# A hand-laid order of steps for pooled attention and an MLP mixer, laid out anew for units 0 to 7

## The chip, the cores and the metric

The kernel runs on one core of a Trainium2 chip. The metric is the device time of one execution in microseconds; three executions give a median. The profile is of one further execution.

## The reference

Eight batches, eight heads, 576 rows, head dimension 64. Keys and values are first averaged over groups of 8 rows (72 groups), then attention runs over the 72 pooled rows. The result, laid out as 576 x 512 for each batch, goes through a mixer: a token part (576 to 256 to 576 along the rows) with a residual, then a channel part (512 to 1536 to 512) with a residual.

```python
k_p = k.reshape(B, H, Sp, 8, D).mean(axis=3);  v_p = v.reshape(B, H, Sp, 8, D).mean(axis=3)
attn = softmax(scale * q @ k_p.T)                      # 576 x 72 for each head
x = (attn @ v_p) as (B, 576, 512)
h = relu(x.T @ w_tok1) @ w_tok2;   u = x + h.T         # token part
out = u + relu(u @ w_ch1) @ w_ch2                      # channel part
```

## The kernel before, in words

All engines are driven from one list of steps that was written out by hand, and the order in which the program issues instructions is the order in which each engine runs them (`tc.manual_schedule`). There is a head (the string `HEAD`) that loads weights and batch 0, computes batch 0's attention and warms TensorE, and then nine units, 0 to 8. Unit n computes the channel part of batch n for 512 of its 576 rows; unit 8 does the remaining 64 rows of all eight batches together.

A unit is a generator (`unit_fast`) that issues a little TensorE work and yields, 45 times in units 0 to 6. Yields 0 to 23 are the first layer (`l1_tile`, L551): 12 tiles of four 512-column matmuls, two for each yield, each tile evicted by ScalarE with a ReLU into `GT` (L555). Yields 24 to 44 are the second layer in seven products of 12 matmuls of 256 columns (L699), three yields each. They follow a scheme with seven instead of eight block products: VectorE forms sums of blocks of `GT` (steps `=1` to `=4`, L579 and L594, into the tile `area`), and, once in unit 0, sums of blocks of `w_ch2` (steps `w0` to `w3`, L579, into `area2`, which the trace also calls area). The products are, in order, x, y, z, x again (needs `=1` to be read by z, and `=2`), w, z again (needs `=4`), x a third time (needs `=3` and `w2`). Each ends in VectorE adds (L742, tiles `s` and `o`); the x, y, z, w banks are four one-bank PSUM tiles, `p1a` to `p1d`, taken and given back in turn, and the steps below share them. Units 7 and 8 do the first layer in a seven-product scheme too (`l1_fast`, L672), with sums of `w_ch1` (steps `Z0` to `Z3`, on POOL) and of the transposed u (steps `y` on VectorE, `Y` on POOL).

`PLAN[n]` says which steps of later batches are issued after which yield of unit n. A step is written batch dot name:

- `lq`, `lk`, `lv`: POOL issues the load of q, k, v of that batch (L162, L124). Raw tiles have two buffers each.
- `K0 K1 V0 V1`: POOL pools half of the heads of k or v in three adds (L208, L209, L212 or L214). `k0 k1 v0 v1`: the same on VectorE.
- `1.vpool0`, `1.vpool1`: batch 1's values are pooled by six matmuls each (L144, `add_rows`; batch 1 is in `WIDE`, six rows for each partition), and cast by VectorE (L295).
- `Q0 Q1`: VectorE transposes q (`qD`, L312). `kpT`: TensorE transposes the pooled keys (L256), ScalarE copies them (L258).
- `s0 s1 s2`: scores (L325) into both buffers of the two-bank PSUM tile `p`, exponentials on ScalarE (L334).
- `av0` to `av4`: attention times values (L413) into one buffer of `p`; VectorE takes reciprocals (L417) and scales (L356). `aw`: the same with the scaling on ScalarE in eight pieces (L360).
- `at0 at1`: the token part's first layer (L425, ReLU L427). `u0` to `u4`: its second layer (L447, `u4` L442) and the residual add on VectorE (L448). `t0` to `t3`: transposes of u on TensorE (L456, copy L457) for the first layer of the next unit.
- From batch 3 on the transposes go another way: `M0 M2 M4` spill u to HBM from SP's queue (L466), `M` and `MT` read it back in another order (L478), and `T0` to `T5` are block transposes on VectorE (L490).
- `g`: a gate. VectorE writes a flag (L865) and POOL copies it (L866), so POOL does not go on before VectorE has come to that place. There is one flag, so VectorE's next gate also waits until POOL has copied the last one.

Of the kernel before, what the change touches and what calls it, by code (L numbers as in the profile page):

```python
# [19 lines left out]

HEAD = """LkA LkT LkB LvT Lq LvA LvB Lt1 Lk1 Lt2 Lc1b Lc1a Lq1 Lc1c Lv1 Lc1d p1 Lc2a Lc2b Lc2c d2 d2 d3 d1 d4 d4 c0 c1 prep q0 kp0 kp1 kt0 q1 d1 o0 kt1 kp2 e0 e1 q3 kt2 o1 q2 e3 vpool0 o3 e2 a00 vpool1 a02 o2 m01 d1 d1 m00 a04 X1 m03 a14 m02 X0 m04 p0 a10 a12 1.kpool m10 m14 m12 m13 m11 A1 A0 X2 X3 A2 A3"""
PLAN = [
# [9 lines left out]
]  # L32

# [907 lines left out]
```

## Time and profile before

| | |
|---|---|
| median of 3 runs | 262.4 us (262.34 to 263.7) |
| the profiled execution | 261.59 us, span 259.8 us |
| PE (TensorE) busy | 253.5 us (98%) |
| DVE (VectorE) busy | 195.3 us (75%) |
| ACT (ScalarE) busy | 125.1 us (48%) |
| POOL (GpSimd) busy | 159.2 us (61%) |
| mean granted TensorE clock | 0.997 |
| first matmul of units 0 to 8 | 23.65, 55.64, 85.75, 113.47, 142.91, 167.19, 194.03, 218.63, 237.00 us |

The busy time of PE counts matmuls whose ends are modelled and overlap the next, so it is read here for gaps only. A row of the timeline gives start, length, engine, line, operation, tile written from tiles read, and in brackets the idle time of the engine before it and what ended it.

### The profile page before, as it was taken

The numbers are of one execution on the slowest core, as the hardware profiler recorded it, in microseconds if no ns is written. First come the engines' busy times: TensorE is split into PE (matmuls) and PEld (weight loads), VectorE is DVE, ScalarE is ACT, GpSimd is POOL, SyncE is SP. The second block draws the span as 40 slices with busy tenths as digits, with TensorE's granted clock in tenths as the row PEclk, the third lists the DMA queues.
The fourth block names the chain that finished last, engine by engine and source line by source line (L and its number), as shares of the span: only waits on it lengthen the run. The fifth ranks groups of instructions, "written<-read, shape, count | busy, mean of one in ns | idle before, by whom it ended". The sixth has DMA issues, their size and how long they took to land.

```text
span 259.8 us, 5518 instructions
## 1 busy us (share of the span) xinstructions
PE 253.5 (98%) x2187; PEld 167.2 (64%) x2187; DVE 195.3 (75%) x400; ACT 125.1 (48%) x229; POOL 159.2 (61%) x166
## 2 busy tenths in 40 slices
PE   8999999999999999999999999999999999999994
PEld 2885456764676645774487447754784478888883
DVE  5557469995789747789799548944795389999993
ACT  3354874059746565466741575065525421623610
POOL 8757226999989999389969962898308913100000
PEclk9999999999999999999999999999999999999998
DMA  7999999994090989479834942930405042503304
GB/s 153 192 201 207 205 207 209 206 225 87 3 174 7 165 192 200 124 132 237 200 109 78 216 170 61 158 97 1 159 20 149 30 146 61 172 0 68 97 3 161
DMA packets 31930, 34.31 MB, mean 132 GB/s; under 512 B 2976, under 2 KB 23968, under 8 KB 31904
## 3 DMA queue, kind: packets, MB, share of 16 engines
q0 software_dynamic: 17856, 17.64, 43.2%
q1 hardware_dynamic: 13632, 15.93, 20.5%
q10 hardware_dynamic: 416, 0.39, 0.5%
q8 instruction: 17, 0.28, 0.4%
q14 instruction: 9, 0.07, 0.1%
HBM read 38.99 MB, written 12.58 MB: 199 GB/s over the span
## 4 chain that ended last, share of the span: by engine, by line
PE 92%; DVE 5%; issue 1%; ACT 0%; DVEq 0%; ACTq 0%
PE p1a L699 8%; PE p1c L551 8%; PE p1d L699 7%; PE p1a L551 7%; PE p1b L699 7%; PE p1b L551 7%; PE p1d L551 7%; PE p1c L699 5%; PE p L413 4%; PE p L325 3%; PE p L672 2%; PE p1d L425 2%; PE p1c L447 2%; PE p1b L425 2%; PE p1b L144 1%; DVE s L742 1%
## 5 line engine op out<-in xcount | busy, mean ns | idle before, releaser
L551 PEld LDWEIGHTS <-w_ch 128*128 128x128 bf16 x336 | 30.2, 98 | 34.0 <-issue 3.0
L699 PEld LDWEIGHTS <-area 128*128 128x128 bf16 x432 | 41.3, 98 | 7.9 <-issue 1.0
L334 ACT ACTIVATE ex<-p 72x768 bf16<-72x768 f32 x42 | 31.6, 803 | 16.1 <-PE p L325 16.1
L866 POOL COPY flag<-flag 1x1 f32<-1x1 f32 x35 | 10.2, 292 | 47.1 <-DVE flag L865 46.9
L699 PEld LDWEIGHTS <-GT 128*128 128x128 bf16 x312 | 29.6, 98 | 7.0 <-issue 1.8
L209 POOL TENSOR_TENSOR t<-t 72x512 f32<-72x512 f32 x22 | 31.0, 1411 | 1.7
L551 PE MATMUL p1c<-uT,w_ch 128*128 128x512 bf16 x92 | 24.9, 379 | 0.0
L208 POOL TENSOR_TENSOR t<-vr 72x1024 f32<-72x1024 bf16 x11 | 24.0, 2181 | 0.6
L208 POOL TENSOR_TENSOR t<-kr 72x1024 f32<-72x1024 bf16 x11 | 24.0, 2178 | 0.3
L551 PE MATMUL p1a<-uT,w_ch 128*128 128x512 bf16 x84 | 22.6, 380 | 0.0
L551 PE MATMUL p1d<-uT,w_ch 128*128 128x512 bf16 x80 | 22.3, 379 | 0.0
L551 PE MATMUL p1b<-uT,w_ch 128*128 128x512 bf16 x80 | 21.5, 379 | 0.0
L356 DVE TENSOR_TENSOR x<-p,den 128x512 bf16<-128x512 f32 x28 | 19.4, 692 | 1.0
L555 ACT ACTIVATE GT<-p1a 128x512 bf16<-128x512 f32 x21 | 12.7, 605 | 14.3 <-issue 7.2
L555 ACT ACTIVATE GT<-p1c 128x512 bf16<-128x512 f32 x23 | 13.9, 603 | 8.1 <-PE p1c L551 8.1
L555 ACT ACTIVATE GT<-p1b 128x512 bf16<-128x512 f32 x20 | 12.1, 604 | 8.8 <-PE p1b L551 5.2
L413 PEld LDWEIGHTS <-ex 72*128 72x128 bf16 x280 | 12.8, 98 | 5.3 <-DVE xt L356 0.7
L555 ACT ACTIVATE GT<-p1d 128x512 bf16<-128x512 f32 x20 | 12.0, 600 | 6.9 <-PE p1d L551 6.1
L579 DVE TENSOR_TENSOR area<-GT 128x1536 bf16<-128x1536 bf16 x9 | 11.0, 1218 | 5.6 <-ACT AT L427 5.1
L413 PE MATMUL p<-vp,ex 72*128 72x65 bf16 x280 | 14.0, 194 | 0.2 <-DVE xt L356 0.2
L448 DVE TENSOR_TENSOR u<-p1c,x 128x512 bf16<-128x512 f32 x11 | 8.0, 730 | 7.9 <-PE p1c L447 7.6
L594 DVE TENSOR_TENSOR area<-GT 128x1536 bf16<-128x1536 bf16 x9 | 9.1, 1016 | 6.1 <-ACT GT L555 5.8
(244 smaller groups left out, 550.3 us busy)
## 6 DMA issues: line engine op xcount, KB each, us to landing
out_dram<-o SPq DMA_DIRECT2D x32, 256.0 KB, 4.1
qb<-in_q_dram POOLq DMA_DIRECT2D x7, 576.0 KB, 10.8
kr<-in_k_dram POOLq DMA_DIRECT2D x6, 512.0 KB, 10.7
vr<-in_v_dram POOLq DMA_DIRECT2D x6, 512.0 KB, 11.7
w_ch<-in_moe_w_ch_dram POOLq DMA_DIRECT2D x5, 512.0 KB, 16.5
mem<-u SPq DMA_DIRECT2D x10, 256.0 KB, 2.2
v<-mem SPq DMA_DIRECT2D x20, 128.0 KB, 2.8
area<-in_q_dram SPq DMA_DIRECT2D x2, 288.0 KB, 3.1
```

Of the source, the lines that this page charges most:

```text
L208: eng.tensor_tensor(out=t4[:, 0:n], in0=t[:, hs, 0:4], in1=t[:, hs, 4:8], op=ALU.add)
L209: eng.tensor_tensor(out=t4[:, 0:n, 0:2], in0=t4[:, 0:n, 0:2], in1=t4[:, 0:n, 2:4], op=ALU.add)
L334: nc.scalar.activation(out=dst, in_=src, func=AF.Exp, scale=scale)
L356: nc.vector.tensor_tensor(out=dst, in0=view, in1=den[:, :, :, None].broadcast_to([n, a, 4, D]), op=ALU.mult)
L413: nc.tensor.matmul(out=ps[:, h // 4, (h % 4) * (D + 1):(h % 4 + 1) * (D + 1)], lhsT=st["ex"][:, h * S + n0:h * S + n0 + P], rhs=st["vp"][: ...
L425: nc.tensor.matmul(out=ps, lhsT=w_tok1[:, c if c < 4 else 4 + par, m * P:(m + 1) * P], rhs=st["x"][:, c, :] if c < 4 else st["xt"], start= ...
L551: nc.tensor.matmul(out=ps, lhsT=w_ch1[:, kk, m * P:(m + 1) * P], rhs=uT[kk], start=(kk == 0), stop=(kk == 3))
L555: nc.scalar.activation(out=GT[:, :, m, :], in_=ps.rearrange("p (h n) -> p h n", h=2), func=AF.Relu)
L579: eng.tensor_tensor(out=out, in0=a, in1=b, op=ALU.subtract)
L594: eng.tensor_tensor(out=S[0], in0=g[1][0], in1=g[1][1], op=ALU.add)
L699: nc.tensor.matmul(out=ps[i] if split else ps[:, i], lhsT=chunk(u, i, a(m)), rhs=w(m), start=start and m == 0 and (i == 0 or split), stop= ...
L866: nc.gpsimd.tensor_copy(out=flag[:, 1:2], in_=flag[:, 0:1])
```

## The change

`HEAD` stays, and so do all functions. The rows of `PLAN` for units 0 to 7 are replaced; unit 8's row stays. The steps are the same, in another order, but for one: the second half of the pooling of batch 7's values (`7.V1` on POOL) becomes `7.v1` on VectorE. There are 37 gates in place of 35. Some steps change the unit: `2.v1` goes from unit 1 to the end of unit 0; `3.Q0` from unit 0 to 1; `3.av0`, `4.Q0` and `5.lk` from unit 1 to 2; `4.aw2` and `6.lq` from unit 2 to 3; `7.lv`, `6.av0` and `5.u4` from unit 4 to 5.

```diff
 PLAN = [
-    {0: "0.u0 2.lk 0.u1 1.Q0 1.Q1", 2: "1.kpT", 3: "3.lq 2.lq", 5: "0.u3", 6: "1.s0", 7: "0.u2", 8: "2.lv", 9: "1.s1", 11: "1.vpool1", 12: "1.s2 1.vpool0", 13: "=3 g", 14: "1.av2", 15: "1.av1", 17: "1.aw0", 18: "1.av4 g", 19: "w0", 20: "3.lv 1.av3", 22: "w1", 23: "g =1 =2 3.lk", 25: "1.at1 1.at0 =4", 26: "g 2.K1", 27: "2.K0", 28: "w3", 29: "2.V0", 33: "1.u0", 34: "1.u1", 35: "1.u2", 36: "w2", 37: "2.Q1 1.t2", 40: "1.u3", 41: "1.t0", 42: "1.t3", 43: "g 1.t1 3.Q0 2.Q0 1.u4"},
-    {0: "2.kpT", 1: "2.v1", 3: "2.s0", 8: "3.K1 2.s2", 9: "3.K0", 11: "4.lq", 12: "2.s1", 15: "3.Q1", 16: "2.aw3", 17: "2.av1", 18: "g", 20: "2.av0", 21: "2.av4", 23: "2.av2 =1", 24: "4.lk", 25: "g", 26: "3.kpT 2.at1", 27: "=2", 28: "2.at0 =4 g", 31: "2.u3 4.Q1", 32: "3.s2", 33: "2.t3 2.u2", 35: "3.s0 3.V1", 36: "=3", 37: "3.V0", 38: "g 2.u1", 39: "4.lv 3.s1 2.u0", 40: "5.lk", 41: "4.Q0 2.t2 2.t0", 43: "2.t1 3.av0 3.av2"},
-    {4: "4.K1", 6: "3.av3 3.av4", 9: "3.av1 4.K0", 12: "g 3.at1", 13: "6.lk", 14: "=3 3.at0", 18: "4.kpT 4.V1", 19: "3.u1 4.V0", 20: "3.u0 3.u3", 21: "3.u2 3.u4", 23: "4.s2", 24: "3.M0 3.M2", 25: "=1", 26: "3.M4", 27: "=2", 28: "4.s0", 29: "=4", 30: "3.M", 31: "4.s1 3.MT 3.T3 3.T0", 32: "g 5.lq 5.lv", 34: "3.T1", 35: "4.av4 4.aw1", 36: "3.T2", 38: "g 6.lq", 40: "g", 42: "4.aw2 6.lv"},
-    {1: "4.av0", 3: "5.K1", 5: "4.av3", 8: "4.at1", 9: "4.at0 5.k0", 10: "5.Q0", 11: "4.u2", 12: "5.V0", 13: "4.u1", 15: "5.kpT 4.u3 5.V1", 16: "4.M2", 17: "5.s0", 18: "=3 5.Q1", 19: "6.Q0", 22: "4.u0", 23: "5.s1", 24: "4.M0", 25: "3.T4 =1 3.T5", 26: "=2", 27: "=4", 28: "g", 29: "4.M", 30: "5.s2", 32: "5.av0", 35: "5.av2", 37: "5.av1", 40: "5.av3 5.av4", 42: "4.T3 4.T1 4.T0", 43: "4.T2 5.at0 5.at1"},
-    {2: "6.K1", 5: "7.lq 7.lk 5.u3", 6: "5.u2", 8: "5.u0", 10: "6.K0", 11: "6.kpT", 12: "5.u1 6.V1 6.V0", 13: "5.M0", 16: "6.s0", 17: "5.M2", 18: "5.M", 20: "7.Q1", 21: "7.Q0", 22: "6.Q1 g", 23: "=1", 24: "6.s1 =3", 26: "g", 28: "=2", 29: "6.s2 5.T1", 30: "g", 32: "g 7.lv 5.T3", 34: "5.T0 =4", 36: "g", 37: "g", 41: "5.T2", 42: "6.av3", 44: "6.av0 5.u4"},
-    {0: "7.K0", 2: "6.av2", 6: "6.av1", 7: "6.av4", 8: "7.K1", 9: "6.at0 7.V1 g", 10: "7.kpT g", 12: "=3", 13: "6.at1 g", 14: "g", 17: "6.u3 7.V0", 18: "6.u1", 20: "g 6.u2 7.s0", 21: "6.u0", 24: "7.s1", 25: "=1", 27: "=2 6.M2", 32: "7.av1", 33: "6.M0 =4", 35: "6.M", 36: "7.s2", 37: "g", 39: "6.T0 6.T2", 40: "g", 41: "6.T3", 42: "6.T1", 44: "7.av2 g 7.av3"},
-    {1: "Z0", 4: "7.av0", 6: "7.av4", 8: "7.at1", 10: "Z1", 15: "7.at0", 16: "Z2", 17: "7.u1 7.u0 7.M0 7.u3 7.u4", 19: "7.u2", 20: "=3 Z3", 22: "7.M2", 25: "g =1", 27: "=2 7.M", 28: "g", 33: "=4", 34: "g", 35: "g 7.T3", 37: "7.T1 7.M4 7.T2", 38: "7.T0", 42: "7.y0", 43: "g 7.y1", 44: "7.Y2"},
-    {0: "g", 6: "7.MT", 12: "7.Y3", 18: "g", 21: "=1", 27: "=2", 30: "=3", 32: "=4", 34: "7.T4", 35: "7.T5", 40: "8.y0", 41: "8.y1 8.y3", 42: "8.y2"},
+    {1: "1.Q0 0.u1", 2: "1.kpT 0.u2", 3: "2.lk 2.lq", 6: "0.u0 2.lv 1.s0", 7: "1.Q1", 9: "3.lq 0.u3 1.s1", 10: "1.vpool1", 12: "g 1.s2 1.vpool0", 13: "=3", 14: "1.av1 1.av2", 15: "g", 16: "1.aw0", 17: "1.av4", 19: "w0", 20: "3.lv", 21: "1.av3", 22: "w1", 23: "g =1 =2 3.lk", 24: "g", 25: "1.at1 =4", 26: "2.K1", 27: "1.at0 2.K0", 28: "w3", 30: "2.V0", 33: "1.u0 1.u1", 34: "2.Q1 1.u2", 37: "1.t2", 40: "w2 1.u3 1.t0", 42: "1.t3", 43: "1.t1 2.Q0 g 1.u4", 44: "2.v1 g"},
+    {0: "2.kpT", 4: "2.s0", 5: "3.Q0", 8: "2.s2", 9: "3.K0", 11: "3.K1", 12: "2.s1", 13: "4.lq", 14: "g", 16: "3.Q1 2.aw3", 17: "2.av1", 20: "2.av0", 21: "2.av4", 23: "2.av2", 24: "4.lk =1", 26: "3.kpT 2.at1", 27: "=2 2.at0", 28: "g", 29: "3.V1", 30: "2.u3", 31: "=4 4.Q1", 32: "3.s2", 33: "2.t3 2.u2", 35: "=3 3.s0", 37: "3.V0", 38: "g 2.u1", 39: "3.s1 4.lv 2.u0", 41: "2.t2", 42: "2.t0 2.t1", 43: "3.av2"},
+    {0: "3.av0", 3: "4.Q0", 4: "3.av4 5.lk 4.K1", 8: "g 3.av3", 9: "4.K0", 10: "6.lk", 11: "3.av1", 15: "4.V1", 16: "3.at0 3.at1", 17: "4.V0", 18: "4.kpT =3 3.u0", 19: "3.u1 4.s1", 20: "3.u3", 21: "3.M0 3.u2", 23: "3.u4", 24: "3.M2 4.s2", 25: "=1", 26: "3.M4", 27: "=2", 28: "4.s0", 29: "3.M =4", 30: "3.T0", 32: "g", 34: "5.lq 5.lv", 35: "4.aw1 3.T1 3.T2 3.MT", 36: "4.av4", 37: "3.T3", 38: "g g", 44: "6.lv"},
+    {0: "6.lq", 3: "4.av0", 4: "5.K1 4.aw2", 5: "4.av3", 6: "5.k0", 7: "5.Q0", 8: "4.at1", 9: "4.at0", 12: "5.V0", 13: "4.u1", 15: "4.u2 5.kpT", 16: "=3", 17: "4.u3", 18: "5.Q1 5.s0", 20: "6.Q0", 22: "4.u0 5.V1 4.M0", 23: "5.s1", 24: "4.M2", 25: "3.T4 =1 3.T5", 26: "=2", 27: "=4", 28: "g", 29: "4.M", 30: "5.s2", 32: "5.av0", 34: "5.av4", 37: "5.av1", 38: "5.av2", 40: "5.av3 4.T2", 42: "4.T3 4.T0", 43: "5.at0 4.T1", 44: "5.at1"},
+    {2: "5.u0", 3: "6.K1", 8: "5.u3", 9: "6.K0 7.lq 6.V0", 10: "7.lk", 11: "6.kpT", 13: "5.u2 5.u1", 14: "6.V1", 17: "g 5.M0 5.M2", 18: "6.s0 5.M", 20: "7.Q1 =3", 21: "7.Q0 6.Q1", 24: "6.s1", 25: "=1 g", 28: "g", 29: "=2", 30: "5.T1", 31: "=4", 32: "5.T3 g 6.s2 5.T0", 34: "g", 36: "g", 42: "5.T2 6.av3"},
+    {0: "7.lv 6.av0", 1: "5.u4 6.av2", 3: "7.K0", 6: "6.av1", 7: "6.av4", 8: "7.K1", 9: "6.at0 g 7.v1", 10: "g", 13: "6.at1", 15: "g", 16: "=3 7.V0 7.kpT", 17: "6.u3", 18: "6.u1", 20: "7.s0 6.u2 g", 21: "6.u0", 23: "7.s1", 25: "=1", 27: "=2", 28: "6.M2", 32: "7.av1 g", 33: "6.M0 =4", 36: "7.s2", 37: "g", 38: "6.M", 39: "6.T0 6.T2", 40: "g", 41: "g", 42: "6.T3 6.T1", 44: "7.av2 g 7.av3"},
+    {0: "Z0", 4: "7.av0", 6: "7.av4", 8: "7.at1", 12: "Z1", 15: "7.at0", 17: "7.u1 7.u0 7.u3", 18: "Z2", 19: "7.u2", 20: "=3 Z3", 21: "7.M0 7.u4", 22: "7.M2", 23: "g", 25: "=1 7.M", 26: "=2", 28: "g", 29: "g", 31: "g", 33: "=4 g", 35: "g 7.T3", 36: "7.T0", 37: "7.T1 7.T2", 39: "7.M4", 43: "7.y0 7.y1", 44: "7.Y2"},
+    {0: "g", 2: "7.Y3", 13: "7.MT", 18: "g", 19: "=1", 28: "=2 =3", 31: "=4", 35: "7.T4", 36: "7.T5", 38: "8.y0", 41: "8.y1 8.y3", 44: "8.y2"},
     {21: "=1", 26: "=2", 29: "=4", 32: "=3"},
 ]
 
```

## The prediction

> **What bounds the kernel now.** I read the page's busy line, then the chain that ended last, then the stages.
>
> ```profile
> span 259.8 us, 5518 instructions
> PE 92%; DVE 5%; issue 1%; ACT 0%; DVEq 0%; ACTq 0%
> 23.65:55.64 31.99, 31.64 (x268) 19.43 (x267) 25.03 (x45) 17.15 (x34) 17.64 (x20) 1.00 1.23 206
> 55.64:85.75 30.11, 29.88 (x296) 18.42 (x294) 23.54 (x38) 20.69 (x40) 28.05 (x28) 1.00 0.46 86
> 237.00:259.80 22.80, 18.87 (x170) 16.33 (x167) 18.35 (x36) 7.28 (x13) 0.00 (x0) 0.97 0.32 93
> sum 236.15, PE 231.64 PEld 152.14 DVE 181.16 ACT 115.14 POOL 141.51; mean PE 25.74 PEld 16.90 DVE 20.13 ACT 12.79 POOL 15.72
> ```
>
> TensorE (PE) is 92% of the chain. The stage rows are units 0, 1 and 8 (start and end, length, then busy time of PE, PEld, DVE, ACT, POOL), the sum is over units 0 to 8: in 236.15 us PE is idle for 4.5, and 3.9 of that is unit 8, which keeps its plan. The granted clock is 1.00, so a faster array is not to be had. VectorE (DVE), 181 of 236, is the only other engine near its limit.
>
> So an order can win only where PE stands between two matmuls. I went through the starts of PE's matmuls for gaps over the usual pitch (0.216 us for 512 columns).
>
> ```profile
> 26.54 0.86 PE p1b L551 x4
> 38.24 0.59 PE L551 MATMUL p1d<-uT,w_ch 128*128 128x512 bf16 x2
> 39.00 0.43 PE L413 MATMUL p<-vp,ex 72*128 72x65 bf16 x8 [0.17 <-DVE xt L356]
> 50.59 0.40 PE L456 MATMUL p1d<-ident,u 128*128 128x128 bf16 x4 [0.18 <-DVE u L448]
> 81.95 0.59 PE L447 MATMUL p1b<-AT,w_tok 128*128 128x512 bf16 x2 [0.23 <-DVE flag L865]
> 134.10 0.43 PE L413 MATMUL p<-vp,ex 72*128 72x65 bf16 x8
> ```
>
> Four matmuls take 0.86, so two begun at 38.24 are through at 38.67, and `1.av3` begins at 39.00: 0.33 lost. In this way I count six gaps in units 0 to 7, the first at 39.00, the last at 134.10 (0.08): 0.33, 0.12, 0.34, 0.30, 0.24, 0.08, in all 1.41 us. That is the most an order of units 0 to 7 can gain: 0.54%.
>
> **The change, part by part.** The PE steps are the same set, so PE's work is the same to the matmul. One pooling changes its engine, gates go from 35 to 37, the rest is order.
>
> *`7.V1` becomes `7.v1` on DVE.* Prices: the three adds of `2.v1`. Cover: DVE's idle time ahead of `7`'s place.
>
> ```profile
> 57.15 1.81 DVE L208 TENSOR_TENSOR t<-vr 72x1024 f32<-72x1024 bf16 x1
> 59.00 1.64 DVE L209 TENSOR_TENSOR t<-t 72x512 f32<-72x512 f32 x1
> 60.67 0.83 DVE L214 TENSOR_TENSOR vp<-t 72x256 bf16<-72x256 f32 x1
> 177.85 0.95 DVE L579 TENSOR_TENSOR area<-GT 128x1536 bf16<-128x1536 bf16 x1 [5.14 <-ACT AT L427]
> ```
>
> 4.28 us go into a hole of 5.14, and the sum behind it (`=3`, now yield 16) stays near 178. Cost 0; without that hole it would delay `=3` and the u adds by 4.28, still 30 yields before `=3` is read.
>
> *Unit 0, the av steps.* `1.av1` and `1.av2` now stand together at yield 14, the next two a yield earlier.
>
> ```profile
> 35.03 0.42 PE L413 MATMUL p<-vp,ex 72*128 72x65 bf16 x8
> 36.65 0.69 DVE L356 TENSOR_TENSOR x<-p,den 128x512 bf16<-128x512 f32 x1
> ```
>
> The first begins at 35.03 as before. DVE still scales them one behind the other (second result at 37.34, the end of the row, the first 0.84 earlier), and two PSUM tiles are all there is. PE would reach `1.aw0` at 35.03 + 2 x 0.27 + 2 x 0.43 = 36.43 and `1.av4` at 37.26: it waits about 0.14 at each. `1.av3` at yield 21 finds its tile free. Net +0.28 - 0.33 = -0.05.
>
> *Unit 0, `w2` from yield 36 to 40.* This is the term that decides. What a DVE sum of two bf16 tiles does beside a POOL add is seen in unit 1:
>
> ```profile
> 78.36 2.12 POOL L208 TENSOR_TENSOR t<-vr 72x1024 f32<-72x1024 bf16 x1
> 79.16 2.14 DVE L579 TENSOR_TENSOR area<-GT 128x1536 bf16<-128x1536 bf16 x1
> 80.56 1.88 POOL L209 TENSOR_TENSOR t<-t 72x512 f32<-72x512 f32 x1
> ```
>
> The sum alone takes 0.95 (row 177.85). Here it begins 0.80 into POOL's add, gets going when that ends (80.48) and ends at 81.30; POOL's next add then waits for the sum. Now unit 0's end:
>
> ```profile
> 44.00 1.24 POOL L124 DMA_DIRECT2D kr<-in_k_dram  x2 [1.21 <-DMA kr<-in_k_dram]
> 45.42 0.83 POOL L866 COPY flag<-flag 1x1 f32<-1x1 f32 x1 [0.19 <-DVE flag L865]
> 45.26 0.95 DVE L579 TENSOR_TENSOR area<-w_ch,area 128x1536 bf16<-128x1536 bf16 x1
> 46.22 2.11 POOL L208 TENSOR_TENSOR t<-kr 72x1024 f32<-72x1024 bf16 x1
> 49.75 0.84 POOL L212 TENSOR_TENSOR kp<-t 72x256 bf16<-72x256 f32 x1
> 50.44 0.97 DVE L579 TENSOR_TENSOR area<-w_ch 128x1536 bf16<-128x1536 bf16 x1
> 50.67 2.73 POOL L208 TENSOR_TENSOR t<-kr 72x1024 f32<-72x1024 bf16 x1
> 52.02 0.65 DVE L742 TENSOR_TENSOR s<-p1c,u 128x512 f32<-128x512 f32 x1
> 53.22 0.60 PE L699 MATMUL p1a<-area,area 128*128 128x256 bf16 x4
> ```
>
> Before, `w2` (50.44) slips in between POOL's L212 (ends 50.59) and the next L208, which it delays. After, it stands behind the `s4` add (52.02, some 0.15 earlier there as two DVE instructions ahead of it are gone) and begins at 51.9. POOL's L208, no longer delayed, runs from 50.67 to 52.78. `w2` gets through at 53.6. Its reader is the last product of unit 0 (before at 53.22; after, without waits, 53.0): PE waits 0.55. Queued behind `w2` on DVE is `1.u3`'s add, for which `1.t3` then waits some 0.2 more. Bounds: 0, if `w2` meets no POOL add (row 50.44); up to 1.8, if it begins just after one of 2.1 us. I take 0.75, near the row 79.16. The trace agrees with a rule of the Trainium skill ("SBUF — State Buffer", Who interferes with whom): a VectorE instruction with two SBUF inputs and a GpSimd instruction that reads SBUF exclude each other, and whoever issues first holds the port for its whole instruction. By that rule alone the collision is certain; by row 50.44 alone unit 0 would end 0.75 earlier.
>
> The u and t steps from yield 33 lose 0.33 in place of 0.46 (row 50.59: `2.Q1` now runs before `1.u2`'s add, but `1.u1` is a yield earlier). Unit 0 in sum: -0.05 + 0.75 - 0.13, about **+0.6**.
>
> *Units 1 and 2.* `=3` of unit 1 moves up a yield and meets the end of a POOL add, not its first half; the gap at 81.95 shrinks from 0.30 to 0.1. `4.s1` leaves the end of unit 2, and with it the gap of 0.24 there. Against that, `3.T0` moves to yield 30, ahead of `s5`:
>
> ```profile
> 104.60 3.72 SPq L478 DMA_DIRECT2D v<-mem  x8
> 108.99 0.77 DVE L490 STREAM_TRANSPOSE uT<-v 128x256 uint32<-128x256 uint32 x2 [1.62 <-DMA v<-mem]
> ```
>
> DVE already waits 1.62 us here for the bounce through HBM, with `s5` behind it. `3.u2` and so the bounce come about 0.9 later, `s5` about 0.6 later, just when PE wants it; the last transpose (`3.T3`) ends as unit 3 begins. 0 to 0.6; I take 0.3. Sum -0.2 - 0.24 + 0.3, **-0.15**.
>
> *Unit 3.* `4.aw2` goes into the row `4.av0`, `4.aw2`, `4.av3` of three neighbouring yields on two PSUM tiles: 0.2. And POOL issues `6.lv` ahead of `6.lq`:
>
> ```profile
> 113.31 0.72 POOL L162 DMA_DIRECT2D qb<-in_q_dram  x1
> 114.15 1.27 POOL L124 DMA_DIRECT2D vr<-in_v_dram  x2
> 126.38 1.43 DVE L312 STREAM_TRANSPOSE qD<-qb 128x576 uint32<-128x576 uint32 x2
> 128.72 0.73 DVE L448 TENSOR_TENSOR u<-p1b,x 128x512 bf16<-128x512 f32 x1 [0.91 <-PE p1b L447]
> DMA to landing us min/median/max: 6.7/9.3/11.9
> ```
>
> The last row is of the two q loads in this stretch; 113.31 + 11.9 = 125.2, and `6.Q0` is the second of the transposes at 126.38. Issued 2.3 us later and behind v, `6.lq` lands near 129, and DVE stands at `6.Q0` for 1.5 us, with `4.u0`'s add, `=1`, `=2`, `=4` and the av scalings behind. Ahead of that add DVE is idle for 0.91 now (row 128.72), so some 0.6 of the 1.5 is left as delay on DVE, which is then busy up to the unit's end; it comes to PE through the av tiles and the last transposes of the unit, and I take 0.4 (0 to 1.2). With two small gaps of before gone (0.15), **+0.45**.
>
> *Loads and spills.* In unit 0 POOL issues `2.lq` and `2.lv` ahead of `3.lq`; `3.lk` still comes last and still waits for `2.lk`'s landing (row 44.00, 1.21), so POOL's first pooling of batch 2 can begin no earlier. `2.lv` lands sooner and `3.lq` later, both far ahead of use. In unit 3 SP gets `4.M0` ahead of `4.M2` and waits at it for `4.u0`; the bounce comes 0.4 later with some 4 us to spare. 0.
>
> *Units 4 to 7.* `6.K0` and `6.V0` come earlier, batch 5's tail (`5.u4`) moves from unit 4 into unit 5 with its work; every gate's POOL copy is done before DVE's next gate writes the flag. I find no wait: 0, with -0.2 to +0.3.
>
> Sum: 0.6 - 0.15 + 0.45 = 0.9, against the profiled execution of 261.59 us (span 259.8 and 1.8 around it): 262.5. The median of the three runs, 262.4, lies 0.8 above that execution; on it the forecast is **263.2 us** (0.8 of the 0.9 taken, as the small terms are rounded up).
>
> **The rivals.**
> 1. *POOL takes the port first (slower).* POOL's issue of `3.lk` ends at 44.00 + 1.24 = 45.24. In the new order gate and `2.K1` stand ahead of `w3`, whose DVE queue reaches it near 45.14. If the load lands 0.15 earlier, or DVE comes 0.15 later, `2.K1`'s L208 begins first and `w3` waits until 47.5; `oa`, `s5` and three u adds queue behind, and PE, which needs their PSUM tiles from 47.4 on, loses about 1.4 there and 1.0 at `w2`, less the 0.2 that the other terms of unit 0 save; with 0.3 from units 1 to 3, +2.5: 264.9. For it: a margin of 0.1 us. Against: before, the copy at 45.42 was held by `w3` in just this way. The skill's same section says that issue order decides who blocks.
> 2. *The new waits are absorbed.* `w2` finds a gap, or `6.lq` lands in time: -0.2, 262.2.
> 3. *The order does what an order can.* All gaps but a tenth go: 262.4 - 1.3 = 261.1. Against it: the rows of `w2`.
> 4. *The bounce in unit 2 comes a full 1 us late*, and unit 3 cannot begin: +1.6, 264.0.
>
> **How the numbers follow.** Forecast 0.40 (262.5 to 264.2), rival 1 0.25 (264 to 266), rival 2 0.20, rival 3 0.08, rival 4 0.07. A half per cent is 1.3 us, about what a measurement of this kernel can tell from no change; so faster means under 261.1, slower over 263.7. Faster: most of rival 3, 0.06. Slower: rival 1, most of rival 4, and a fifth of the forecast, 0.39. The rest, 0.55, is the same. Range 261.4 to 265.4: it leaves out the far ends of rivals 1 and 3. Without rival 1 the forecast's own range is 262.5 to 264.2.
>
> **What would show it.** Right: in unit 0 a row DVE L579 near 51.9 of 1.5 us or more, and PE's last product there after 53.5; in unit 3 the second qD transpose waiting for a DMA near 128; unit 4 beginning 0.5 to 1.2 us later. Rival 1: L579 near 45.2 over 2 us. Wrong: unit 0 ending before 55.64, or a new PE gap in units 4 to 7, where I found none.

## The result, and the profile after

| | before | after |
|---|---|---|
| median of 18 runs each on the same chip | 262.10 us (261.59 to 263.70) | 264.42 us (262.87 to 269.66) |
| the profiled execution | 261.59 us, span 259.8 | 264.25 us, span 262.5 |

The changed kernel takes 1.0081 times as long, 95% interval 1.0058 to 1.0104, that is 2.1 us more; the ratios here and below leave disturbed runs out (of the changed kernel's 18 the three from 267.55 us up, whose granted clock was 0.991 to 0.994). It is slower by more than the half per cent that the prediction set as its line. The other 15 lie between 262.87 and 266.31 us, a wider spread than before. Below, before and after name the two kernels, and a row is quoted by its start.

The chain that ended last in the changed kernel, then its stages: units 0 to 5 and the sum over all nine units (start and end, length, then busy time of PE, PEld, DVE, ACT, POOL).

```profile
PE 71%; DMA 13%; DVE 9%; issue 3%; POOL 2%; ACT 0%; DVEq 0%; ACTq 0%; POOLq 0%
```

```profile
23.51:58.47 34.96, 32.48 (x263) 19.16 (x266) 26.63 (x44) 17.06 (x34) 19.07 (x21) 1.00 1.17 195
58.47:88.10 29.63, 29.36 (x283) 18.16 (x286) 20.73 (x37) 20.69 (x40) 26.53 (x28) 1.00 0.43 81
88.10:115.60 27.50, 27.34 (x238) 16.79 (x239) 19.92 (x38) 14.78 (x29) 22.65 (x22) 1.00 0.79 167
115.60:145.62 30.02, 29.65 (x259) 17.90 (x260) 26.53 (x50) 14.86 (x30) 24.27 (x19) 1.00 0.63 140
145.62:168.98 23.36, 23.31 (x184) 14.46 (x185) 15.83 (x35) 12.22 (x20) 13.56 (x19) 1.00 0.66 143
168.98:196.73 27.75, 27.59 (x245) 17.05 (x246) 22.34 (x48) 12.95 (x21) 16.04 (x17) 1.00 0.38 97
sum 238.95, PE 231.46 PEld 151.51 DVE 185.00 ACT 115.38 POOL 138.19; mean PE 25.72 PEld 16.83 DVE 20.56 ACT 12.82 POOL 15.35
```

The same view of the kernel before, units 2 to 5 (units 0 and 1 stand in the prediction):

```profile
85.75:113.47 27.72, 27.72 (x240) 16.87 (x238) 19.57 (x37) 14.07 (x28) 22.34 (x22) 1.00 0.78 160
113.47:142.91 29.44, 29.44 (x255) 17.77 (x252) 26.20 (x50) 15.48 (x34) 25.81 (x21) 1.00 0.76 162
142.91:167.19 24.28, 24.28 (x197) 14.91 (x197) 16.39 (x36) 11.90 (x20) 15.76 (x18) 1.00 0.66 143
167.19:194.03 26.84, 26.84 (x236) 16.75 (x235) 17.72 (x43) 13.03 (x21) 15.82 (x18) 1.00 0.28 80
```

Compare lengths, not busy times (the trace of after lacks 24 matmul records). Unit 0 lasts 34.96 in place of 31.99: **+2.97**. Units 1 to 3 together -0.12 (-0.48, -0.22, +0.58; two av steps of 0.27 moved from unit to unit among them). Units 4 and 5 trade a step and batch 5's tail: -0.92 and +0.91. Units 6 and 7 are equal and unit 8 is 0.04 shorter. So the 2.7 us between the two profiled executions are unit 0.

Inside unit 0, the timeline of after:

```profile
41.85 0.96 DVE L579 TENSOR_TENSOR area<-w_ch,area 128x1536 bf16<-128x1536 bf16 x1 [0.54 <-DMA w_ch<-in_moe_w_ch_dram]
44.63 0.06 DVE L865 MEMSET flag<- 1x1 f32 x1
45.06 1.25 POOL L124 DMA_DIRECT2D kr<-in_k_dram  x2 [1.32 <-DMA kr<-in_k_dram]
46.20 3.17 DVE L579 TENSOR_TENSOR area<-w_ch,area 128x1536 bf16<-128x1536 bf16 x1
46.30 0.17 POOL L866 COPY flag<-flag 1x1 f32<-1x1 f32 x1
46.44 2.11 POOL L208 TENSOR_TENSOR t<-kr 72x1024 f32<-72x1024 bf16 x1
49.29 0.68 DVE L742 TENSOR_TENSOR o<-p1b,s 128x512 f32<-128x512 f32 x1
50.02 0.59 PE L447 MATMUL p1b<-AT,w_tok 128*128 128x512 bf16 x2 [1.85 <-DVE o L742]
51.26 0.38 PE L447 MATMUL p1d<-AT,w_tok 128*128 128x512 bf16 x1 [0.21 <-DVE u L448]
54.63 1.14 DVE L579 TENSOR_TENSOR area<-w_ch 128x1536 bf16<-128x1536 bf16 x1
```

The sum `w3` takes 3.17 us where it took 0.95: it stands until POOL's L208 ends (48.55). The `o` add behind it gives a PSUM bank back 3.2 us later than before (46.13 there), and PE waits for it. This is rival 1. `w2`, the forecast's own term, is only 0.2 over: with everything before it late, it meets the last 0.3 of a POOL add.

Not all of the 2.97 is the order. In this execution the sum `w1` (row 41.85) waited 0.54 for the last load of `w_ch`, which landed 19.4 us after its issue (18.3 in the trace before); DVE, and so `w3`, came later by that. The 13% of DMA in the chain lead through this load. In f4 below, a run with the same row of `PLAN` for unit 0, `w1` did not wait, and unit 0 lasted 34.37. In f2, with the unit 0 of before, `w1` waited 0.33, so the late landing does not need the new order.

What the gate did stands in one row of the kernel before, beside the copy at 45.42 in the prediction:

```profile
45.28 0.06 DVE L865 MEMSET flag<- 1x1 f32 x1
```

There the memset stood next to `w3` on DVE, and POOL could not go on before DVE had come to it. After, the memset is done at 44.63, and only the issue of `3.lk` holds POOL.

### The profile page after: what moved, and what is told of

It is laid out like the page before. It is cut to its first block, busy times and chain, and to the rows that moved or that the text cites. A ratio compares the mean times of both kernels' runs of the same rounds, so it can differ in the third digit from the quotient of the medians.

```text
span 262.5 us, 5503 instructions
## 1 busy us (share of the span) xinstructions
PE 252.4 (96%) x2163; PEld 166.3 (63%) x2187; DVE 199.1 (76%) x405; ACT 125.4 (48%) x229; POOL 155.7 (59%) x165
## 4 chain that ended last, share of the span: by engine, by line
PE 71%; DMA 13%; DVE 9%; issue 3%; POOL 2%; ACT 0%; DVEq 0%; ACTq 0%; POOLq 0%
DMA w_ch<-in_moe_w_ch_dram 7%; PE p1b L699 7%; PE p1d L551 6%; PE p1b L551 6%; PE p1c L699 6%; PE p1c L551 6%; PE p1a L699 6%; PE p1a L551 5%; PE p1d L699 5%; DMA area<-in_moe_w_tok_dram 3%; PE p L325 3%; PE p L413 3%; DMA qb<-in_q_dram 2%; PE p L672 2%; DVE area L579 2%
## 5 line engine op out<-in xcount | busy, mean ns | idle before, releaser
L209 POOL TENSOR_TENSOR t<-t 72x512 f32<-72x512 f32 x21 | 28.5, 1359 | 1.6
L551 PE MATMUL p1b<-uT,w_ch 128*128 128x512 bf16 x90 | 24.8, 379 | 0.1
L551 PE MATMUL p1d<-uT,w_ch 128*128 128x512 bf16 x87 | 24.3, 379 | 0.2
L208 POOL TENSOR_TENSOR t<-kr 72x1024 f32<-72x1024 bf16 x11 | 23.4, 2124 | 0.4
L208 POOL TENSOR_TENSOR t<-vr 72x1024 f32<-72x1024 bf16 x10 | 21.8, 2184 | 1.4 <-DMA vr<-in_v_dram 1.0
L551 PE MATMUL p1c<-uT,w_ch 128*128 128x512 bf16 x77 | 22.0, 379 | 0.3
L356 DVE TENSOR_TENSOR x<-p,den 128x512 bf16<-128x512 f32 x28 | 19.4, 691 | 1.0
L551 PE MATMUL p1a<-uT,w_ch 128*128 128x512 bf16 x68 | 18.6, 378 | 0.1
L555 ACT ACTIVATE GT<-p1d 128x512 bf16<-128x512 f32 x23 | 13.9, 605 | 9.8 <-PE p1d L551 9.4
L448 DVE TENSOR_TENSOR u<-p1a,x 128x512 bf16<-128x512 f32 x12 | 8.7, 726 | 9.9 <-PE p1a L447 8.6
L417 DVE RECIPROCAL den<-p 128x8 f32<-128x8 f32 (+1 forms) x35 | 7.0, 200 | 9.7 <-PE p L413 9.2
L124 POOL DMA_DIRECT2D vr<-in_v_dram x15 | 9.5, 637 | 7.7 <-DMA vr<-in_v_dram 3.4
```

Source lines behind the costliest of these rows:

```text
L124: nc.gpsimd.dma_start(out=t[j0:j1, h0:h1].rearrange("j h i d -> j h (i d)"), in_=src[b, h0:h1].rearrange("h (j i) d -> j h (i d)", i=POOL) ...
L208: eng.tensor_tensor(out=t4[:, 0:n], in0=t[:, hs, 0:4], in1=t[:, hs, 4:8], op=ALU.add)
L209: eng.tensor_tensor(out=t4[:, 0:n, 0:2], in0=t4[:, 0:n, 0:2], in1=t4[:, 0:n, 2:4], op=ALU.add)
L356: nc.vector.tensor_tensor(out=dst, in0=view, in1=den[:, :, :, None].broadcast_to([n, a, 4, D]), op=ALU.mult)
L448: nc.vector.tensor_tensor(out=rows_of(c), in0=blocked(ps), in1=blocked(x), op=ALU.add)
L551: nc.tensor.matmul(out=ps, lhsT=w_ch1[:, kk, m * P:(m + 1) * P], rhs=uT[kk], start=(kk == 0), stop=(kk == 3))
```

## The experiments

All are differences in `PLAN`; steps are quoted with their yields. Medians of all runs, with the ratio to the kernel before on the same chip. Unit 0 is that of the one profiled execution:

| run | us | ratio, 95% interval | unit 0, us |
|---|---|---|---|
| e1: after, gate back at 26 | 264.01 | 1.0047 (1.0022 to 1.0072) | 33.32 |
| e2: before, gate at 24 | 263.37 | 1.0044 (1.0025 to 1.0062) | 33.29 |
| e3: after, `w2` back at 36 | 263.93 | 1.0060 (1.0037 to 1.0084) | 33.44 |
| e4: before, `7.v1` on DVE | 263.42 | 1.0038 (1.0024 to 1.0053) | 31.99 |
| f1: after, gate and `w2` back | 263.97 | 1.0057 (1.0024 to 1.0090) | 34.13 |
| g1: f1, `2.Q1` back | 262.55 | 1.0026 (0.9998 to 1.0053) | 32.65 |
| g3: before, `2.Q1` ahead of `w2` | 263.44 | 1.0038 (1.0017 to 1.0058) | 33.26 |
| h1: f1, a gate at `w2` | 262.76 | 1.0021 (1.0000 to 1.0042) | 32.02 |
| f2: before's unit 0, rest of after mended | 262.18 | 0.9996 (0.9976 to 1.0015) | 32.16 |
| f3: e4, `7.kpT` later | 262.36 | 0.9995 (0.9977 to 1.0013) | 32.00 |
| f4: after, units 3 and 4 mended | 263.77 | 1.0055 (1.0037 to 1.0073) | 34.37 |
| g2: all named steps mended | 262.38 | 0.9999 (0.9981 to 1.0017) | 32.19 |

**e2, the gate alone, in the kernel before.**

```diff
-25: "1.at1 1.at0 =4", 26: "g 2.K1",
+24: "g", 25: "1.at1 1.at0 =4", 26: "2.K1",
```

> The kernel before with only that gate moved the other way, from yield 26 to 24 of unit 0; no other step moves. Theory 1: POOL is through with the issue of 3.lk when VectorE comes to w3, the copy and 2.K1's first add go first, w3 takes about 3.1 us, and 1.2 to 2.0 us are lost: 263.3 to 264.1. Theory 2 and theory 3: no change, 262.1.

```profile
45.00 0.17 POOL L866 COPY flag<-flag 1x1 f32<-1x1 f32 x1
45.14 2.11 POOL L208 TENSOR_TENSOR t<-kr 72x1024 f32<-72x1024 bf16 x1
45.40 2.67 DVE L579 TENSOR_TENSOR area<-w_ch,area 128x1536 bf16<-128x1536 bf16 x1
48.73 0.59 PE L447 MATMUL p1c<-AT,w_tok 128*128 128x512 bf16 x2 [0.46 <-DVE o L742]
```

Two yields for one gate cost 1.0 us in the median and 1.30 in unit 0. `w3` is held as in after; `w2`, late in its turn, meets a POOL add too and takes 1.49, of which PE loses 0.24. The mechanism is shown in the kernel before, with nothing else changed.

**e1, the gate put back in the changed kernel.**

```diff
-24: "g", 25: "1.at1 =4", 26: "2.K1",
+25: "1.at1 =4", 26: "g 2.K1",
```

> The changed kernel with unit 0's second gate moved from yield 24 to 26, where it stood before: its flag is then written behind the s1 add, directly ahead of w3. Theory 1 (POOL's first add of 2.K1 takes the port ahead of w3): w3 back from 3.17 to about 0.95 us, 1.7 to 2.2 us of the loss gone, 262.2 to 262.8; then w2 at yield 40 should meet a POOL add and cost up to 0.75. Theory 2 (the loss is at w2, the forecast): no change, 264.4. Theory 3 (loads in unit 0 land later): at most 0.3 less.

```profile
46.28 0.95 DVE L579 TENSOR_TENSOR area<-w_ch,area 128x1536 bf16<-128x1536 bf16 x1
46.51 0.77 POOL L866 COPY flag<-flag 1x1 f32<-1x1 f32 x1
51.71 2.12 POOL L208 TENSOR_TENSOR t<-kr 72x1024 f32<-72x1024 bf16 x1
52.87 1.78 DVE L579 TENSOR_TENSOR area<-w_ch 128x1536 bf16<-128x1536 bf16 x1
54.70 0.60 PE L699 MATMUL p1c<-area,area 128*128 128x256 bf16 x4 [0.52 <-DVE area L579]
164.57 0.45 DVE L490 STREAM_TRANSPOSE uT<-v 128x256 uint32<-128x256 uint32 x1 [2.69 <-DMA v<-mem]
166.57 0.60 PE L699 MATMUL p1d<-w_ch,area 128*128 128x256 bf16 x4 [1.78 <-DVE s L742]
```

`w3` is clean, the copy waits for it, and unit 0 is 1.6 shorter than after's. Now the forecast's term appears as drawn: `w2` meets an L208 and takes 0.83 more, PE loses 0.68. The time gives little of it back: the median is 264.01, where 262.2 to 262.8 and up to 0.75 for `w2` were expected. The profiled execution (264.88; the runs reach from 262.30 to 266.99) shows two more losses. PE also stands 0.47 early in unit 0, and here `5.T1` (unit 4, moved ahead of `=4` and its adds) waited 2.69 us for the read-back of the bounce, whose slowest landing took 4.7 us (3.1 in after): unit 4 took 25.46 in place of 23.36. One profile does not tell how much of this is in the median.

**e3, `w2` put back, the gate left.**

```diff
-34: "2.Q1 1.u2", 37: "1.t2", 40: "w2 1.u3 1.t0",
+34: "2.Q1 1.u2", 36: "w2", 37: "1.t2", 40: "1.u3 1.t0",
```

> The changed kernel with w2 back at yield 36 of unit 0, the gate as changed. Theory 1: w3 still blocked for 3.1 us and the main loss stays; 0.0 to 0.3 us less than 264.4, as w2 met the end of a POOL add at 54.63 and took 1.14 instead of 0.95. Theory 2: 0.75 less, 263.7.

`w2` took 0.93, `w3` still 2.98. The median lies between the two theories, and its ratio cannot be told from after's. Unit 0 is 33.44, 1.5 shorter than in after, but the place of `w2` gives only 0.27 of that (PE ahead of its matmuls at 55.83 and 56.48 in after). 0.81 is a shorter wait for the bank behind `w3` (1.20 lost there, 2.01 in after, 1.46 in f4), and the rest comes earlier in the unit. The gate's collision stays.

**f1, both put back.** The edits of e1 and e3 together.

> The changed kernel with both unit 0 terms undone: the gate stands again ahead of 2.K1 at yield 26, w2 again at yield 36. Everything else of the new order stays. Theory 1 (nearly all of the loss is the two port collisions in unit 0): w3 takes 0.95 us, w2 takes 0.95 to 1.0, unit 0 lasts 32.0 to 32.5 us (34.96 in the profile of the changed kernel, 31.99 before), and the time is 262.0 to 262.6, that is within 0.2% of the kernel before. Theory 2 (the rest of the new order costs about 1 us as well): unit 0 as short, but the time 263 or more, with the loss seen in units 3 and 4.

Neither theory foresaw this: unit 0 took 34.13.

```profile
50.29 0.76 DVE L312 STREAM_TRANSPOSE qD<-qb 128x576 uint32<-128x576 uint32 x1
51.83 2.12 POOL L208 TENSOR_TENSOR t<-kr 72x1024 f32<-72x1024 bf16 x1
52.17 2.59 DVE L579 TENSOR_TENSOR area<-w_ch 128x1536 bf16<-128x1536 bf16 x1
55.41 0.38 PE L456 MATMUL p1b<-ident,u 128*128 128x128 bf16 x4 [1.54 <-DVE s L742]
```

At its old yield `w2` comes 0.34 behind POOL's start, as the transpose `2.Q1` (0.76) stands ahead of it; before, that stood behind. So there is a third step in unit 0.

**g3, that step alone, in the kernel before.**

```diff
-35: "1.u2", 36: "w2", 37: "2.Q1 1.t2",
+35: "2.Q1 1.u2", 36: "w2", 37: "1.t2",
```

> The kernel before with one step moved: 2.Q1 from yield 37, behind w2, to yield 35, ahead of 1.u2's add and w2. If order on VectorE decides who gets the port: the transpose of 0.76 puts w2 behind the start of GpSimd's second pooling, w2 takes 2.3 to 2.7 us in place of 0.97, the last adds and transposes of unit 0 come 1.3 to 1.8 later, time 263.6 to 264.1. If GpSimd comes as much later as VectorE does, or w2 is not on the path: 262.2 to 262.8.

```profile
50.18 0.76 DVE L312 STREAM_TRANSPOSE qD<-qb 128x576 uint32<-128x576 uint32 x1
51.04 2.12 POOL L208 TENSOR_TENSOR t<-kr 72x1024 f32<-72x1024 bf16 x1
51.46 2.51 DVE L579 TENSOR_TENSOR area<-w_ch 128x1536 bf16<-128x1536 bf16 x1
51.61 0.40 PE L456 MATMUL p1d<-ident,u 128*128 128x128 bf16 x4 [0.83 <-DVE u L448]
54.62 0.38 PE L456 MATMUL p1c<-ident,u 128*128 128x128 bf16 x4 [0.43 <-DVE s L742]
```

`w2` takes 2.51, unit 0 33.26 (+1.27), the time is 1.1 longer, a little under the range expected. Only half of it is the port: PE loses 0.60 at 54.62, behind `w2`. The other 0.64 it loses at 51.61, where it waits for `1.u2`'s add, which stands behind the transpose on DVE. In f1, with `1.u1` a yield earlier, this second wait is small (0.18), and PE loses 1.70 behind `w2`.

**g1, f1 with `2.Q1` back behind `w2`.**

```diff
-34: "2.Q1 1.u2", 36: "w2", 37: "1.t2",
+34: "1.u2", 36: "w2", 37: "2.Q1 1.t2",
```

> The changed kernel with three steps of unit 0 put back: the gate ahead of 2.K1 at yield 26, w2 at yield 36, and 2.Q1 behind w2 at yield 37 (in the new order it stands at 34). With the first two alone w2 still met GpSimd's second pooling (2.59 us), as 2.Q1's transpose of 0.76 stood ahead of it on VectorE. If that transpose is the reason: w2 takes 0.95 to 1.4 us and GpSimd's add waits for it, the gap of 1.70 ahead of the last transposes of unit 0 goes, unit 0 lasts 32.2 to 32.7 and the time is 262.2 to 263.0. If w2 is late for another reason: w2 1.8 us or more, unit 0 over 33.

`w2` takes 0.94, and POOL's L208 is the one that waits (2.78). Unit 0 is 32.65, and the interval touches no change: 1.0026 is left of after's 1.0081. The three orders on one port are the bulk of the loss. In this execution the port shows in unit 3 too: POOL's add begins 0.05 ahead of DVE's last add of `5.k0`, which takes 2.34 in place of 0.42, and PE stands behind it.

```profile
121.41 2.12 POOL L208 TENSOR_TENSOR t<-vr 72x1024 f32<-72x1024 bf16 x1 [0.53 <-DMA vr<-in_v_dram]
121.46 2.34 DVE L212 TENSOR_TENSOR kp<-t 72x256 bf16<-72x256 f32 x1
125.16 1.02 PE L551 MATMUL p1d<-uT,w_ch 128*128 128x512 bf16 x4 [0.41 <-DVE u L448]
```

**h1, order by a gate in place of order by time.** f1 with `2.Q1` left ahead of `w2`:

```diff
-27: "1.at0 2.K0", 28: "w3", 30: "2.V0", ... 36: "w2",
+27: "1.at0", 28: "w3", ... 36: "g 2.K0 2.V0 w2",
```

> The changed kernel with the gate ahead of 2.K1 at yield 26 and w2 at yield 36 as in the earlier run that still lost 1.70 us at w2 (2.Q1 stays at 34, ahead of w2), and one gate more: it stands directly ahead of w2 on VectorE, and GpSimd's second pooling 2.K0 (and 2.V0) behind it. If a gate beside a sum fixes who gets the port whatever the times: w2 takes 0.95 to 1.0 us, GpSimd's L208 begins behind it, the gap of 1.70 goes (2.K0's result is later and 2.kpT may wait up to 0.6), unit 0 lasts 32.4 to 32.9 in place of 34.13, time 262.4 to 263.2. If the collision is a matter of when VectorE comes, not of order: w2 over 2 us again and 263.5 or more.

```profile
51.12 0.94 DVE L579 TENSOR_TENSOR area<-w_ch 128x1536 bf16<-128x1536 bf16 x1
51.13 0.06 DVE L865 MEMSET flag<- 1x1 f32 x1
51.27 0.84 POOL L866 COPY flag<-flag 1x1 f32<-1x1 f32 x1 [0.56 <-DVE flag L865]
52.07 2.11 POOL L208 TENSOR_TENSOR t<-kr 72x1024 f32<-72x1024 bf16 x1
```

One gate beside the sum takes unit 0 from 34.13 to 32.02, less than expected even. Of these 2.11 the gate's part is 1.62 (PE's loss behind `w2` falls from 1.70 to 0.08); another 0.47 is a wait for a load early in f1's unit 0, which this execution did not have. The gain over g1 does not last: unit 1 takes 30.45 after g1's 29.70. POOL's poolings end no earlier than there (the L212 of `2.K0` begins at 55.61, in g1 at 55.51), and PE, which is now 0.68 ahead, waits 0.28 and 0.45 for the pooled keys of batches 2 and 3. POOL's queue is what is late next. The Trainium skill ("SBUF — State Buffer", Who interferes with whom) says that the one that issues first keeps the shared pair for its whole instruction and the other blocks. The runs agree that the other blocks: in the four profiles with the gate at 24 (after, e2, e3, f4) `w3` took 2.67 to 3.24, in the ten others 0.95.

**e4 and f3, the pooling on DVE, in the kernel before.**

```diff
-9: "6.at0 7.V1 g", 10: "7.kpT g",                     # before
+9: "6.at0 7.v1 g", 10: "7.kpT g",                     # e4
+9: "6.at0 7.v1 g", 10: "g", ... 16: "7.kpT",          # f3
```

> The kernel before with only 7.V1 on VectorE as 7.v1, at the same place. All theories: 4.28 us of VectorE work in a hole of 5.14, no change (262.1, within 0.2). If it costs, then =3 behind it ends later than 30 yields allow, which the trace of before speaks against.

> The kernel before with 7.V1 on VectorE (7.v1, which alone cost about 1.0 us) and, besides, 7.kpT moved from yield 10 to 16. Theory A (VectorE's pooling adds hold the port, GpSimd's last add of 7.K1 waits for them, and the transposes 7.kpT wait for that add): with the transposes behind, the gap of 0.7 in unit 5 goes, unit 5 lasts 26.8 to 26.9 and the time is 262.1 to 262.5, although GpSimd's add still takes about 2 us in place of 0.84. Theory B (the gates and the sum =3 behind 7.v1 are late): the gap stays, unit 5 27.4 or more and 263.2 or more.

e4 and then f3:

```profile
173.22 2.01 POOL L212 TENSOR_TENSOR kp<-t 72x256 bf16<-72x256 f32 x1
173.34 1.20 DVE L208 TENSOR_TENSOR t<-vr 72x1024 f32<-72x1024 bf16 x1
175.29 0.24 PE L256 MATMUL p1c<-ident,kp 72*128 72x72 bf16 x2 [0.54 <-POOL kp L212]
```

```profile
173.06 2.04 POOL L212 TENSOR_TENSOR kp<-t 72x256 bf16<-72x256 f32 x1
178.04 0.30 PE L256 MATMUL p1c<-ident,kp 72*128 72x72 bf16 x4
```

No theory expected e4 to cost anything, and it is 1.1 slower. DVE's adds have room, but they take the port from POOL's last add of `7.K1`, for which `7.kpT` waits: unit 5 lasts 27.55 in e4 (26.84 before). With the transposes six yields later POOL's add is as slow and nobody waits: unit 5 26.84, and the time that of the kernel before. Theory A holds.

**f2, f4, g2: what the rest is worth.** The mends, besides those named (in f2 `2.v1` and `3.Q0` also stand in the units where they stood before):

```diff
-unit 2: 38: "g g", 44: "6.lv"     unit 3: 0: "6.lq"
+unit 2: 38: "g g 6.lq"            unit 3: 0: "6.lv"
-unit 4: 30: "5.T1", 31: "=4", 32: "5.T3 g 6.s2 5.T0"
+unit 4: 31: "=4", 32: "5.T1 5.T3 g 6.s2 5.T0"
-unit 0: 1: "1.Q0 0.u1", ... 10: "1.vpool1"            # g2 only
+unit 0: 1: "0.u1 1.Q0", ... 11: "1.vpool1"            # g2 only
```

> Unit 0 of the kernel before, units 1 to 8 of the changed kernel, with two steps of these mended: 6.lq is issued ahead of 6.lv again, and 5.T1 stands behind =4 and its s5 (yield 32 in place of 30). If unit 0 is the whole loss and units 1 and 2 really gain 0.2 each: unit 0 32.0 us, units 1 and 2 29.6 and 27.5, unit 3 without a wait at the second q transpose, time 261.4 to 262.0, a little faster than the kernel before (ratio 0.997 to 0.9995). If the later units of the new order lose what they gain: 262.2 to 263.

> The changed kernel with only its units 3 and 4 mended: 6.lq ahead of 6.lv, 5.T1 at yield 32 behind =4 and s5. Unit 0 keeps both collisions. If the steps of unit 3 and 4 matter: unit 3 lasts 29.7 in place of 30.0, no wait at the second q transpose, and the spread of the runs is smaller, as s5 no longer stands behind a transpose that waits for a bounce; time 263.6 to 264.1. If they are hidden: as the changed kernel, 264.2 to 264.6.

> As the run with the gate, w2 and 2.Q1 put back, and besides: 0.u1's add ahead of the transpose 1.Q0 (which waits up to 1.5 us for its load at the start of unit 0), 1.vpool1 at yield 11, 6.lq ahead of 6.lv, 5.T1 at yield 32. If the sum of the named steps is all that the new order loses, what is left are its small gains: unit 0 31.7 to 32.1 us, units 1 and 2 29.6 and 27.5, time 261.3 to 262.0, faster than both kernels (ratio 0.996 to 0.999). If something else in the new unit 0 costs, it lasts 32.5 or more and the time is 262.3 to 263.

f2 is the kernel before within its interval: units 1 and 2 about as short as expected (29.78, 27.49), unit 3 30.02, where DVE's L212 stood 2.23 against POOL as in g1. f4 shows unit 3 at 29.67 and unit 4 at 23.60, and is still 0.55% slow: unit 0 is the loss. Its read-back landed late too (4.4 us), but with `5.T1` behind `=4` that cost unit 4 only 0.24, not 2.1. Its runs lie within 2.2 us, but whether the two mends or chance made them closer is not settled. g2 missed: 262.38, not 261.3 to 262. Its units 1 to 3 are 29.67, 27.49 and 29.68, but unit 0 is 32.19, with 0.41 lost ahead of the transpose at 53.03. No version beat the kernel before by more than the uncertainty.

## Why the prediction was right, and where it was not

The time lies in the range, slower by more than 0.5%, a case that had 0.39; 0.55 stood on no change, and the likeliest case (263.2) was not the one that came. Without rival 1 the range ended at 264.2, below the 264.4 measured. So the time was right through a rival with a chance of 0.25 and not through the forecast's own sum, which is luck in part.

- **What bounds the kernel, and the ceiling of 1.41.** Nothing speaks against it. PE is the bound, and the best repaired orders (f2, g2) end level with the kernel before; no run came near the ceiling.
- **Unit 0, the port.** The mechanism was right in kind, the place was wrong: +2.97 in place of +0.6. The step that failed is rival 1's weight, "a margin of 0.1 us", and the argument against it, that the copy at 45.42 was held by `w3`. The copy's length was, but its start was not: the row quoted there ends in `[0.19 <-DVE flag L865]`, a wait for the gate. Before, the gate stood beside `w3` and fixed the order; moved two yields, it fixed nothing, and POOL won in all four profiles. The condition that was set for it, 0.15 less margin, was not even met: in after `w3`'s row begins 0.11 ahead of the end of POOL's issue (46.31), about the margin forecast, and loses. Rival 1's price was near: 2.5 forecast, 2.7 between the profiles and 2.1 by the ratio. Of its parts, 1.4 at `w3` were 2.0 (1.5 in f4, where `w1` did not wait for its load) and 0.4 (PE at 50.02 and 51.26), and 1.0 at `w2` was 0.27.
- **`w2` to yield 40, +0.75.** Right as a price: 0.83 on DVE and 0.68 on PE in e1. In after it is masked by the delay ahead of it.
- **The u and t steps.** `2.Q1` was priced by PE's gap alone. That it also pushes `w2` on DVE was missed; in f1 PE loses 1.70 behind `w2`. By itself, in the order of before, the step costs 1.1 (g3), about half of it by each way.
- **The av steps.** Right: the trace of after has PE stand 0.14 ahead of each of `1.aw0` and `1.av4`.
- **Missed in unit 0.** `1.Q0` ahead of `0.u1` puts an add behind a transpose that waits up to 1.5 us for its load. It cost PE 0.16 in after, 0.46 to 0.48 in e1, f1, f4 and g1, where the transpose waited 1.5, and nothing in e3 and h1, where it waited 0.65 and 0.81; with the add first (g2) there is no gap either. `1.vpool1` a yield earlier waited 0.31 in after, in other runs not.
- **Units 1 and 2, -0.15.** -0.43 once the moved av step is taken out (-0.21, -0.22). The 0.3 for `3.T0` ahead of `s5` was not needed.
- **Unit 3, +0.45.** +0.31, but not by the steps named. `6.Q0` waited 0.31 for its load, not 1.5, and in f1 0.74 with unit 3 at 29.67. The loss of after stands with `=1`:

```profile
130.37 0.78 DVE L312 STREAM_TRANSPOSE qD<-qb 128x576 uint32<-128x576 uint32 x1 [0.31 <-DMA qb<-in_q_dram]
132.18 0.72 POOL L214 TENSOR_TENSOR vp<-t 72x256 bf16<-72x256 f32 x1
132.29 1.43 DVE L594 TENSOR_TENSOR area<-GT 128x1536 bf16<-128x1536 bf16 x1
```

  The sum began 0.11 behind a POOL add and took 1.43; DVE was then late for the av tiles, and PE lost 0.23 and 0.12 near 141 and 143. In f1 the same sum began 0.16 ahead and took 0.96. This is read from two traces; no run isolated it. With the sum free, f1's 29.67 is no more than before plus the moved av step (29.71), so the steps named cost nothing there. Unit 3 of before itself lasts 29.42 to 29.65 in the five profiles that keep its order.
- **`7.v1`, cost 0.** Right for the whole change and wrong as reasoned. (At yield 16, `=3` stands 26 yields ahead of its reader, not 30; that is still ample.) The cover that was named, DVE's idle time, was not the one that mattered: alone, the edit costs 1.1 (e4). The changed order hid it by moving `7.kpT` to yield 16 (f3), which the prediction did not price: in after that POOL add took 1.70, and PE did not wait for it.
- **Loads and spills, 0.** The load `3.lk` was issued 1.1 later than before (45.06), and POOL's pooling began no earlier, as said; it began ahead of `w3` all the same, as `w3` came 0.94 later too.
- **Units 4 to 7, 0.** Right in after (-0.01). But `5.T1` ahead of `=4` makes unit 4 hang on a landing; when that is late, it costs 2.1 (e1; 0.24 in f4 with the step behind).

What stays open: how much of after's spread (262.87 to 266.31) comes from such races, and how often each goes which way; only single profiles show them. The order of before has such a race at `w2` too: in f2 `w2` began 0.24 into POOL's L212, took 1.41, and PE lost 0.17.

## What to carry to other kernels

Before a gate or a wait is moved, ask what it orders besides the data it guards: here a one-element flag decided which of two engines got a shared port, and two yields of it cost 1.0 us. Where two instructions that exclude each other come within a few tenths of a microsecond, make their order certain, with the one that the critical engine reads first, and do not treat the nearness as a small chance. Cover for a moved step means more than idle time on its engine: look for whom it blocks elsewhere, and for who waits for that one.

## What the runs showed of the hardware

- The start of a DVE row is not the moment at which it has the port. In after, `w3`'s row begins at 46.20, ahead of POOL's copy (46.30) and L208 (46.44), and still loses: DVE's add before it runs until 46.27 (45.59, 0.68 long). The rows do not tell the winner: in f4 the copy begins 0.09 after the end of that add and POOL wins, in before also 0.09 after it, and `w3` wins. What sets the two apart, other than the gate's place, is not shown.
- A collision costs both sides in turn. In after the L209 that met the released `w3` took 1.87 in place of 1.26, and in g1 POOL's L208 took 2.78 in place of 2.12, each time held by DVE's sum.
- The three pooling adds on DVE took 1.20, 1.21 and 0.42, 2.83 us in all (e4), where the rows used for their price had 4.28: those met POOL's adds. In after the first of them met one too and took 2.01.
- The read-back of the bounce is not steady: its slowest landing in unit 4 took 4.7 us in e1 and 4.4 in f4, and 2.7 to 3.3 in the twelve other profiles.
